# Two stage joints by column pieces, one PSUM pool, and the opening of the last stage in another order

## The chip, the cores and the metric

The kernel runs on one core of a Trainium2 chip. The metric is the device time of one execution in microseconds (us), the median of three runs. Five engines work side by side: PE (TensorE, matmuls; PEld is its weight load), DVE (VectorE), ACT (ScalarE), POOL (GpSimd), and SP, whose queue issues the DMAs. PE writes to PSUM, which has eight banks of 128 x 512 float32.

## The reference

Three layers follow each other; the output of one is the input of the next.

```python
def _attn_ref(r, k, v, w, u):          # 4 batches, 8 heads, 768 steps, 48 wide
    for t in range(S):
        cur = np.einsum('bhd,bhe->bhde', u[None] * kt, vt)
        y[:, :, t] = np.einsum('bhd,bhde->bhe', rt, state + cur)
        state = w[None, :, :, None] * state + np.einsum('bhd,bhe->bhde', kt, vt)
def _moe_ref(x, phi, w1, w2):          # 3072 tokens x 384, 8 experts of 4 slots, F = 1024
    d = softmax of x @ phi over the tokens;  c = softmax of x @ phi over the slots
    slot_input = d.T @ x
    slot_out[e] = np.maximum(slot_input[e] @ w1[e], 0.0) @ w2[e]
    return c @ slot_out
def _moe2_ref(x, w_in, w_out):         # 384 -> 2048 -> 384
    r = np.maximum(x @ w_in, 0.0)
    return (r * r) @ w_out
```

(The two softmax lines are put in words here.)

## The kernel before, in words

The order of every engine's instructions is the order in which the program text emits them (a manual schedule); a wait is put in where two instructions touch the same tile. So what stands earlier in the text on one engine is in front of what stands later, and can hold it up.

**Attention** runs over 16 units (four batches of four head pairs). Its last lines (L890 to L932) are the **first joint**. The last batch's logits lie in the PSUM tile tagged `lg`. Their column maxima over all batches are brought to one row (L900, L902, L903) and spread again (L908, L910), and `fac` (L912, ACT) is the factor by which the sums of earlier batches (`P2[:, 0]`) and of the last one are rescaled. L913 (DVE) rescales `P2[:, 0]`, 385 columns in one instruction; six matmuls for each of three groups of columns (L919) give the last batch's sums, and L921 (DVE, three times) adds them to `P2[:, 1]`. L924 turns the three groups with the 0/1 matrix `sel` into one PSUM tile, L927 copies them as `siT`, and L928 to L932 do the denominators. `turns` (L247 to L276) brings the last unit's outputs into `xn`: the first half of the heads is copied by ACT, the second by DVE (L272). `idle` (L228) issues matmuls whose results nobody reads. Then the PSUM pool is closed and another one opened (L933 to L935).

**The slot stage** (L944 to L1068) does the experts: `up` (L949) reads `siT` in three column groups `kc`, `turn` transposes, `down` (L970) gathers all experts in one PSUM tile `acc`. Beside it DVE rebuilds float32 words of `w_in` and `w_out` (`to_f32`; `wout_f32` in three steps), `wout_high` (ACT, L1009) and `wout_low` (POOL, L1014) split a block of `w_out` into a high and a low part, and `csplit`, `cstack`, `cstack_copy` prepare the slot weights `cTall`.

**The second joint** is L1078 to L1182. `so` is the copy of `acc` (ACT, one instruction), `soT` its product with `sel`. `G(f, ...)` multiplies `soT` with block `f` of `w_in` (128 of its 2048 columns) and stores it in `gst` in a high and a low part (L1097 on ACT, L1098 on DVE). `quarters(q, ...)` does the same for four blocks at once but with 32 rows each (L1106), and eight small transfers on the SP queue per two blocks put their rows into place (`quarters_out`, L1120: four of 16 KB for one block).

**The last stage** is a loop over 96 steps (L1184): three groups of 1024 tokens, 16 blocks `f`, two halves of 512 tokens. For step `i`, `s_h` (L1134) makes the hidden values in PSUM, `s_relu` (ACT, L1145) rectifies them, `s_sq` squares (DVE L1152, or ACT L1150 for steps 2 to 27), `s_hi` (ACT, L1155) rounds the square to its high part `gh`, and `s_lo` (DVE, L1158) leaves the low part `gl`. Nine matmuls of 512 columns (L1229) multiply: three high x `gh`, three low x `gh`, three high x `gl`. `s_h` is issued two steps ahead, `s_hi` and `s_lo` one step ahead. The results leave by L1237 (two halves of 256 columns, ACT and DVE) or, in the last two steps, L1239 (one instruction), and a DMA each (L1240).

```python
    def s_relu(i, c=ALL):
        nc.scalar.activation(fs[i, "hr"][:, c], fs[i, "p"][:, c], AF.Relu)
    def s_hi(i, c=ALL):
        nc.scalar.copy(part(i, "gh")[:, c], fs[i, "gg"][:, c])
    def s_lo(i, c=ALL):
        nc.vector.tensor_tensor(part(i, "gl")[:, c], fs[i, "gg"][:, c], fs[i, "gh"].bitcast(F32)[:, c], ALU.subtract)
```

Of the kernel before, what the change touches and what calls it, by code (L numbers as in the profile page):

```python
# [17 lines left out]
def rwkv_softmoe_ffn(ctx: ExitStack, tc: tile.TileContext, un, wt, ph, w1, w2, w_in, w_out, out):  # L18
# [24 lines left out]
    psum_cm = tc.tile_pool(name="psum_att", bufs=1, space=bass.MemoryType.PSUM)  # L43
    psum = psum_cm.__enter__()
# [3 lines left out]
    BANKS = {"A": 3}  # L48

    def ps(tag, banks=1):  # L50
        cnt[0] += 1
        return psum.tile([128, 512 * banks], F32, name=f"ps_{tag}{cnt[0]}", tag=tag, bufs=BANKS.get(tag, 1))
# [194 lines left out]
    def turns(x, k):  # L247
# [22 lines left out]
        for a in range(2):  # L270
            if x is not None:
                (nc.vector.tensor_copy if a and x == NU - 1 else nc.scalar.copy)(turned(x, a), px[a])  # L272
            if k is not None:
                nc.scalar.copy(kn[:, :4, a], to[a])
# [630 lines left out]
    idle(2, 128, 64)  # L905
    nc.scalar.copy(st["el", B - 1][:, 1], st["lg", B - 1][:96, :256])
# [15 lines left out]
    pv, pd = ps("kv"), ps("lg")  # L922
    for c in range(3):
        nc.tensor.matmul(pv[:, NS * c:NS * (c + 1)], P2[:, 1, 128 * c:128 * (c + 1)], sel[:96, 0],  # L924
                         start=(c == 0), stop=True, skip_group_check=True)
    siT = wk([128, 3, NS], "siT", 1)
    nc.vector.tensor_copy(siT.rearrange("p c s -> p (c s)"), pv[:, :3 * NS])  # L927
# [150 lines left out]
    nc.scalar.copy(so, acc[:, :DM])  # L1078
    cstack(3, "lg")
    wout_f32(2, 0)  # L1080
    p = ps("tr")
    for c in range(3):
        nc.tensor.matmul(p[:, 128 * c:128 * (c + 1)], so[:, 128 * c:128 * (c + 1)], sel.rearrange("p r s -> p (r s)"),
                         start=True, stop=True)
    nc.scalar.copy(soT.rearrange("p c s -> p (c s)"), p[:, :384])
    cstack(4, "kv")
    cstack_copy(3)
    cstack_copy(4, nc.vector.tensor_copy)
    wout_f32(2, 1)
    wout_f32(2, 2)  # L1090

    def G(f, n, tag):
# [3 lines left out]
        g = gst[:, 128 * f:128 * (f + n)]  # L1096
# [63 lines left out]
    G(0, 1, "A")  # L1160
    G(1, 1, "A")
    s_h(0)
    s_h(1)
    G(2, 1, "A")
    quarters(1, "lg")
    first, second = slice(0, 256), slice(256, 512)
    s_relu(0, first)
    s_relu(0, second)
    s_sq(0, first)
    s_hi(0, first)  # L1170
    s_sq(0, second)
    s_lo(0, first)
    s_hi(0, second)
    quarters_high()
    s_relu(1)
    s_lo(0, second)
    quarters_low()
    quarters_out(1, 0)
    s_sq(1)
    G(3, 1, "kv")  # L1180
# [3 lines left out]
    for i, (sg, f, half) in enumerate(order):  # L1184
        if f == 0:
            acc = (acc if half else []) + [[ps(t) for t in atag[half]]]
        if sg == 0 and half == 0:
            wout_f32(f + 3, 0)
        if i + 1 < NI:
            s_hi(i + 1)  # L1190
            s_lo(i + 1)
        if sg == 0 and half == 1:
            wout_f32(f + 3, 1)
        if i + 2 < NI:
            s_h(i + 2)
            s_relu(i + 2)
            s_sq(i + 2)
        if sg == 0 and half == 0:
# [7 lines left out]
        if i in (11, 19):  # L1206
            quarters(2 + i // 19, "tr")
            quarters_high()
            quarters_low()
        for q in range(1, NQ):  # L1210
            at = i - (0, 0, 11, 19)[q]
            if at in ((2, 4, 6) if q == 1 else (0, 2, 4, 6)):
# [88 lines left out]
```

## Time and profile before

| | us |
|---|---|
| median of three runs (376.81 to 377.42) | 377.04 |
| the profiled execution, its own time | 376.01 |
| its span | 374.3 |
| PE busy | 366.4 (98%) |
| DVE busy | 266.6 (71%) |
| ACT busy | 205.4 (55%) |
| POOL busy | 103.7 (28%) |

The span is what the trace covers, and 1.7 us of the execution's own time lie around it. The page gives busy times per engine, the chain that ended last (followed back from the last instruction), and groups of instructions; the trace answers for any stretch which instruction ran when, and what it waited for.

### The profile page before, as it was taken

What the parts mean: (1) busy time and instruction counts of PE and PEld (TensorE: products, weight loads), DVE (VectorE), ACT (ScalarE), POOL (GpSimd) and SP (SyncE); (2) the same over time, 40 slices, a digit from 0 to 9 for tenths busy, and PEclk for the clock granted to TensorE, in tenths of its full rate; (3) what the DMA queues carried; (4) which work ended last, traced back from release to release, by engine and by line L of the source; (5) the groups of instructions that cost most, each with busy time, mean ns of one, the idle gap of its engine ahead of it and who ended that gap; (6) DMA issues with size and microseconds to landing.
All of it is one profiled execution on the core that took longest, in us unless ns stands there. A gap on an engine that the chain in (4) does not pass through costs nothing.

```text
span 374.3 us, 9041 instructions
## 1 busy us (share of the span) xinstructions
PE 366.4 (98%) x3703; PEld 298.7 (80%) x3703; DVE 266.6 (71%) x460; ACT 205.4 (55%) x439; POOL 103.7 (28%) x117
## 2 busy tenths in 40 slices
PE   8999999999999999999999999999999999999995
PEld 6888888988886556887878888888888888888884
DVE  8879878889663694899885767566666765666662
ACT  3244544543632433998887765555555655555553
POOL 3558795587633130352222400000000000000000
PEclk9999999999999999999999999999999999999999
DMA  7999899999999998142332013000000210000004
GB/s 263 411 340 415 301 407 391 406 361 407 332 392 409 409 388 291 34 121 89 106 93 65 7 42 126 3 0 0 2 1 0 100 70 0 2 1 0 2 0 169
DMA packets 22281, 65.09 MB, mean 174 GB/s; under 512 B 2416, under 2 KB 4448, under 8 KB 22240
## 3 DMA queue, kind: packets, MB, share of 16 engines
q1 hardware_dynamic: 22240, 64.52, 46.0%
q8 instruction: 29, 0.48, 0.5%
q14 instruction: 12, 0.10, 0.1%
HBM read 59.00 MB, written 4.72 MB: 170 GB/s over the span
## 4 chain that ended last, share of the span: by engine, by line
PE 97%; DVE 1%; issue 1%; ACT 0%; POOL 0%; POOLq 0%; ACTq 0%
PE ps_A L1229 26%; PE ps_Y L1229 9%; PE ps_kv L1229 9%; PE ps_lg L1229 9%; PE ps_A L306 7%; PE ps_tr L1134 6%; PE ps_YO L336 3%; PE ps_YE L345 3%; PE ps_A L949 3%; PE ps_YO L345 3%; PE ps_Y L970 3%; PE ps_lg L359 2%; PE ps_kv L318 2%; PE ps_YE L269 2%; PE ps_lg L222 1%; PE ps_kv L269 1%
## 5 line engine op out<-in xcount | busy, mean ns | idle before, releaser
L1158 DVE TENSOR_TENSOR slot<-slot,slot 128x512 fp32r<-128x512 f32 (+1 forms) x97 | 71.1, 734 | 53.5 <-PE ps_A L1229 18.6
L1229 PE MATMUL ps_A<-slot,slot 128*128 128x512 f32 x432 | 105.9, 389 | 0.0
L1229 PEld LDWEIGHTS ps_A<-slot,slot 128*128 128x128 f32 x432 | 81.0, 188 | 17.1 <-ACT slot L1155 0.3
L1155 ACT CAST slot<-slot 128x512 fp32r<-128x512 f32 (+1 forms) x97 | 59.7, 616 | 49.5 <-DVE slot L1152 49.1
L1145 ACT ACTIVATE slot<-ps_tr 128x512 f32<-128x512 f32 (+1 forms) x97 | 57.4, 593 | 23.1 <-PE ps_tr L1134 22.1
L1152 DVE TENSOR_TENSOR slot<-slot 128x512 f32<-128x512 f32 (+1 forms) x71 | 48.4, 682 | 11.5 <-ACT slot L1145 11.3
L1229 PE MATMUL ps_Y<-slot,slot 128*128 128x512 f32 x144 | 55.4, 391 | 0.0
L1229 PE MATMUL ps_kv<-slot,slot 128*128 128x512 f32 x144 | 55.1, 389 | 0.0
L1229 PE MATMUL ps_lg<-slot,slot 128*128 128x512 f32 x144 | 55.0, 389 | 0.0
L311 DVE COPY_PREDICATED AT<-mask,ps_A 128x384 f32<-128x384 int32 x63 | 33.6, 586 | 7.5 <-PE ps_A L306 3.2
L1134 PE MATMUL ps_tr<-slot,slot 128*128 128x512 f32 x96 | 37.4, 391 | 0.4 <-DVE slot L1098 0.4
L1014 POOL TENSOR_TENSOR slot<-wf,slot 128x384 fp32r<-128x384 f32 x16 | 20.6, 1288 | 53.2 <-ACT slot L1009 53.2
L295 POOL TENSOR_SCALAR_AFFINE_SELECT AT<-dg 128x768 f32<-128x768 f32 x32 | 28.0, 880 | 20.3 <-DVE dg L288 8.1
L1229 PEld LDWEIGHTS ps_Y<-slot,slot 128*128 128x128 f32 x144 | 27.0, 188 | 5.9 <-issue 0.4
L1229 PEld LDWEIGHTS ps_kv<-slot,slot 128*128 128x128 f32 x144 | 27.0, 188 | 5.7
L1229 PEld LDWEIGHTS ps_lg<-slot,slot 128*128 128x128 f32 x144 | 27.0, 188 | 5.5
L306 PE MATMUL ps_A<-slot 48*128 48x128 f32 x378 | 30.3, 288 | 0.0
L236 DVE TENSOR_TENSOR slot<-slot,ps_tab 112x768 f32<-112x768 f32 (+1 forms) x34 | 29.8, 891 | 0.0
L306 PEld LDWEIGHTS ps_A<-slot 48*128 48x128 f32 x378 | 24.5, 187 | 4.9 <-issue 3.2
L1134 PEld LDWEIGHTS ps_tr<-slot,slot 128*128 128x128 f32 x96 | 17.9, 188 | 4.3 <-DVE slot L1098 0.6
L284 POOL TENSOR_TENSOR slot<-slot,slot 128x576 f32<-128x576 f32 x13 | 18.4, 1417 | 7.6 <-ACT slot L276 7.5
L348 ACT COPY xT<-ps_YE 112x384 f32<-112x384 f32 x16 | 7.7, 479 | 23.4 <-PE ps_YE L345 23.4
(208 smaller groups left out, 529.1 us busy)
## 6 DMA issues: line engine op xcount, KB each, us to landing
slot<-in_un_dram SPq DMA_DIRECT2D x12, 1344.0 KB, 7.3
slot<-in_w_dram SPq DMA_DIRECT2D x24, 512.0 KB, 8.5
slot<-in_w_dram SPq DMA_DIRECT2D x8, 1536.0 KB, 9.7
slot<-in_w_in_dram SPq DMA_DIRECT2D x4, 1536.0 KB, 8.8
wo<-in_w_out_dram SPq DMA_DIRECT2D x16, 384.0 KB, 3.3
out_dram<-slot SPq DMA_DIRECT2D x18, 256.0 KB, 2.4
slot<-in_un_dram SPq DMA_DIRECT2D x9, 448.0 KB, 6.5
slot<-slot SPq DMA_DIRECT2D x48, 16.0 KB, 1.8
```

The lines of the kernel that those rows point to most:

```text
L236: nc.vector.tensor_tensor(x, x, t.unsqueeze(1).to_broadcast(list(x.shape)), ALU.mult)
L295: nc.gpsimd.affine_select(out=at, in_=dg.unsqueeze(3).to_broadcast([128, 2, HC, 128]), pattern=[[0, 2], [0, HC], [1, 128]], compare_op=ALU ...
L306: nc.tensor.matmul(p[h][:, i], tv[rows, 1, 2 * i + par], tv[rows, 0, 2 * i + par], start=True, stop=True)
L311: nc.vector.copy_predicated(st[n, "AT", par][:, h], mask.unsqueeze(1).to_broadcast([128, HC, 128]), p)
L345: nc.tensor.matmul(p[o:o + D, i], vv[:, 2 * i + par, h], at[:, h, i], start=False, stop=True, skip_group_check=True)
L1014: nc.gpsimd.tensor_tensor(wout_half(wls, f, 5), st.pop(("wf", f)), hi, ALU.subtract)
L1134: nc.tensor.matmul(p, gst[:, 128 * f:128 * (f + 1)], cTall[:, 512 * g:512 * (g + 1)], start=True, stop=True)
L1145: nc.scalar.activation(fs[i, "hr"][:, c], fs[i, "p"][:, c], AF.Relu)
L1152: nc.vector.tensor_mul(gg, hr, hr)
L1155: nc.scalar.copy(part(i, "gh")[:, c], fs[i, "gg"][:, c])
L1158: nc.vector.tensor_tensor(part(i, "gl")[:, c], fs[i, "gg"][:, c], fs[i, "gh"].bitcast(F32)[:, c], ALU.subtract)
L1229: nc.tensor.matmul(o, (hi, lo, hi)[k][:, 128 * j:128 * (j + 1)], (gh, gh, gl)[k], start=(f == 0 and k == 0), stop=(f == NF - 1 and k == 2))
```

## The change

First joint: `xn`'s first half is copied by DVE and its second by ACT (before: the other way round). One of two `idle` matmuls before L908 is left out. `P2[:, 0]` is rescaled by ACT in three column groups; the copy of the logits (L906) is moved behind that. The three `sel` products go to three PSUM tiles and are copied one by one by ACT. There is one PSUM pool for the whole kernel: the tag `tr` of the later stages takes the banks `YE` and `YO` in turn, `Y` takes the bank `tab`.

Second joint: `so` and `soT` are made in three pieces. Only blocks 0 and 1 come from `G`; blocks 2 and 3 now come from `quarters(0)` and eight small transfers, and `quarters(1)` moves from the joint into step 3 of the loop. `G` is split: the store of block 1 (`G_out`) comes after step 0's rectifying. `cstack_copy(4)` moves from DVE to ACT and to a later place, `wout_f32(2, 1)` and `(2, 2)` to later places. Step 0: DVE writes the high part straight from the rectified values while ACT makes the square (`s_first`), and its first three matmuls are split into two halves of 256 columns. Step 2's `s_h`, `s_relu` and `s_sq` (`s_ahead`) come between the matmuls of step 0, and in later steps ahead of `wout_high`.

End: the last output tile leaves in two halves (ACT and DVE).

```diff
-    idle(2, 128, 64)
-    nc.scalar.copy(st["el", B - 1][:, 1], st["lg", B - 1][:96, :256])
+    idle(1, 128, 64)
...
-    nc.vector.tensor_scalar(P2[:, 0], P2[:, 0], fac[:, 0:1], None, ALU.mult)
     cols = [slice(0, 128), slice(128, 256), slice(256, DM + 1)]
+    siT = wk([128, 3, NS], "siT", 1)
+    for c in cols:
+        nc.scalar.activation(P2[:, 0, c], P2[:, 0, c], AF.Copy, scale=fac[:, 0:1])
+    nc.scalar.copy(st["el", B - 1][:, 1], st["lg", B - 1][:96, :256])
...
+    for c, tag in enumerate(("kv", "lg", "A")):
+        p = ps(tag)[:, :NS]
+        nc.tensor.matmul(p, P2[:, 1, 128 * c:128 * (c + 1)], sel[:96, 0], start=True, stop=True)
+        nc.scalar.copy(siT[:, c], p)
+    pd = ps("kv")
...
+    for c in range(3):
+        nc.scalar.copy(so[:, 128 * c:128 * (c + 1)], acc[:, 128 * c:128 * (c + 1)])
...
+        p = ps("A")[:, :128]
+        nc.tensor.matmul(p, so[:, 128 * c:128 * (c + 1)], sel.rearrange("p r s -> p (r s)"), start=True, stop=True)
+        (nc.scalar.copy if c == 1 else nc.vector.tensor_copy)(soT[:, c], p)
...
+    def s_first(c):
+        nc.vector.tensor_mul(part(0, "gh")[:, c], fs[0, "hr"][:, c], fs[0, "hr"][:, c])
+        nc.scalar.activation(fs[0, "gg"][:, c], fs[0, "hr"][:, c], AF.Square)
...
+    G(0, 1, "Y")
+    wout_f32(2, 1)
+    quarters(0, "lg")
     s_h(0)
     s_h(1)
...
+    G(1, 1, "Y")
     s_relu(0, first)
     s_relu(0, second)
...
+    s_first(first)
+    s_first(second)
+    G_out(1)
+    s_relu(1)
     s_lo(0, first)
...
+    s_lo(0, second)
+    s_sq(1)
     quarters_high()
...
     quarters_low()
...
+    quarters_out(0, 2)
+    quarters_out(0, 3)
+    cstack_copy(4)
+    wout_f32(2, 2)
     wout_high(1)
     wout_low(1)
...
-        if i in (11, 19):
-            quarters(2 + i // 19, "tr")
+        if i in (3, 11, 19):
+            quarters(1 + (3, 11, 19).index(i), "tr")
...
+        if i == 0:
+            for c in (first, second):
+                for j in range(NJ):
+                    nc.tensor.matmul(acc[0][j][:, c], hi[:, 128 * j:128 * (j + 1)], gh[:, c], start=(c is first),
+                                     stop=False, skip_group_check=True)
+            mms = mms[NJ:]
...
+            if i == 0 and k == 2 and j == 0:
+                s_ahead(2)
...
-                if i < NI - 2:
+                if i < NI - 2 or (i == NI - 1 and j == NJ - 1):
```

PE's order at the first joint, in the kernel before, from the spreading of the maxima (`m`) to the first `up`; lines carry the numbers of their own program, and numbers behind a name count tiles:

```order
L908 MATMUL ps_kv_2067<-ones,m_193_2055 96x2
L919 MATMUL ps_YE_116<-xn_86,en_2061 32x128 x6
L919 MATMUL ps_YO_117<-xn_86,en_2061 32x128 x6
L919 MATMUL ps_A_2074<-xn_86,en_2061 32x129 x6
L924 MATMUL ps_kv_2096<-sel,P_144 128x32 x3
L928 MATMUL ps_lg_2097<-P_144,sel 128x1
L949 MATMUL ps_A_2117<-slot_6_76,siT_2101 32x256 x12
```

The same place in the changed kernel:

```order
L912 MATMUL ps_kv_2065<-ones,m_193_2055 96x2
L926 MATMUL ps_YE_116<-xn_86,en_2061 32x128 x6
L926 MATMUL ps_YO_117<-xn_86,en_2061 32x128 x6
L926 MATMUL ps_A_2076<-xn_86,en_2061 32x129 x6
L931 MATMUL ps_kv_2098<-sel,P_144 128x32
L931 MATMUL ps_lg_2101<-sel,P_144 128x32
L931 MATMUL ps_A_2104<-sel,P_144 128x32
L934 MATMUL ps_kv_2107<-P_144,sel 128x1
L952 MATMUL ps_A_2118<-slot_6_76,siT_2071 32x256 x12
```

The work is the same; the three `sel` products now end in three tiles.

PE's order at the second joint before, from the product that gives `soT` to the first matmul of step 0 (`ps_tr<-slot,slot 128x512` is `s_h`, 32x128 x12 are `quarters`, 128x128 x3 on `slot_220` are `G`):

```order
L1083 MATMUL ps_tr_2440<-sel,slot_258_2428 128x128 x3
L986 MATMUL ps_kv_2445<-ident,cs_2366 128x128 x4
L1095 MATMUL ps_A_2456<-slot_220_2189,slot_258_2428 128x128 x3
L1095 MATMUL ps_A_2462<-slot_220_2189,slot_258_2428 128x128 x3
L1134 MATMUL ps_tr_2468<-slot_234_2256,slot_260_2430 128x512
L1134 MATMUL ps_tr_2470<-slot_234_2256,slot_260_2430 128x512
L1095 MATMUL ps_A_2472<-slot_220_2189,slot_258_2428 128x128 x3
L1106 MATMUL ps_lg_2478<-slot_220_2189,slot_258_2428 32x128 x12
L1095 MATMUL ps_kv_2507<-slot_220_2189,slot_258_2428 128x128 x3
L1134 MATMUL ps_tr_2522<-slot_234_2256,slot_260_2430 128x512
L1229 MATMUL ps_A_2515<-slot_261_2431,slot_253_2384 128x512
```

And in the changed kernel:

```order
L1087 MATMUL ps_A_2449<-sel,slot_260_2429 128x128
L989 MATMUL ps_kv_2452<-ident,cs_2367 128x128 x4
L1095 MATMUL ps_tab_2458<-slot_222_2190,slot_260_2429 128x128 x3
L1110 MATMUL ps_lg_2465<-slot_222_2190,slot_260_2429 32x128 x12
L1138 MATMUL ps_YO_2478<-slot_236_2257,slot_262_2431 128x512
L1138 MATMUL ps_YE_2480<-slot_236_2257,slot_262_2431 128x512
L1095 MATMUL ps_tab_2482<-slot_222_2190,slot_260_2429 128x128 x3
L1244 MATMUL ps_A_2514<-slot_263_2432,slot_255_2385 128x256
```

Two of four `G` products are gone, and one `s_h` stands behind step 0's first matmuls instead of before them.

ACT's order in the changed kernel from step 0's rectifying to step 1's rounding (`L1159`):

```order
L1149 ACTIVATE slot_260_2429<-ps_YO_2478 128x256 x2
L1171 ACTIVATE slot_260_2429<-slot_260_2429 128x256 x2
L1103 CAST slot_262_2431<-ps_tab_2482 128x128
L1149 ACTIVATE slot_260_2429<-ps_YE_2480 128x512
L1115 CAST slot_261_2430<-ps_lg_2465 128x128
L992 CAST slot_236_2257<-ps_kv_2452 128x512
L1012 CAST slot_255_2385<-wf_2389 128x384
L1159 CAST slot_263_2432<-slot_260_2429 128x512
```

The store of block 1 (L1103) and `cstack_copy(4)` (L992) stand between step 0 and step 1 now; the former stood ahead of step 0, the latter on DVE.

## Rows read from the trace of the kernel before

**Rows 1.** The page: the chain that ended last, by engine
```profile
PE 97%; DVE 1%; issue 1%; ACT 0%; POOL 0%; POOLq 0%; ACTq 0%
```
**Rows 2.** Waits of PE inside the span: us in total, times, longest
```profile
PE ps_kv L908 <- DVE m L903: 0.4, 1, 0.4
PE ps_tr L1134 <- DVE slot L1098: 0.4, 1, 0.4
...
PE ps_A L949 <- DVE m L930: 0.2, 1, 0.2
```
**Rows 3.** First joint, timeline: start, us, engine, line, operation, count, idle before
```profile
113.59 0.46 DVE L272 COPY xn<-ps_YO 128x288 f32<-128x288 f32 x1 [0.64 <-ACT xn L272]
113.97 0.23 DVE L902 TENSOR_REDUCE m<-ps_kv 1x32 f32<-1x96 f32 x1
...
115.42 0.42 DVE L913 TENSOR_SCALAR P<-P,m 96x385 f32<-96x385 f32 x1 [0.36 <-ACT m L912]
115.94 0.35 DVE L921 SCALAR_TENSOR_TENSOR P<-ps_YE,m,P 96x128 f32<-96x128 f32 x1
...
116.34 0.93 PE L924 MATMUL ps_kv<-sel,P 96*128 96x32 f32 x6
...
117.72 5.39 PE L949 MATMUL ps_A<-slot,siT 128*32 128x256 f32 x96 [0.25 <-DVE m L930]
```
**Rows 4.** Second joint, timeline of PE, ACT and DVE, from the first G
```profile
144.79 1.60 PE L1095 MATMUL ps_A<-slot,slot 128*128 128x128 f32 x12
...
146.48 0.55 DVE L1098 TENSOR_TENSOR slot<-ps_A,slot 64x128 fp32r<-64x128 f32 x2
...
146.83 0.73 PE L1134 MATMUL ps_tr<-slot,slot 128*128 128x512 f32 x2 [0.43 <-DVE slot L1098]
...
148.26 0.27 ACT L1097 CAST slot<-ps_A 128x128 fp32r<-128x128 f32 x1 [1.56 <-PE ps_A L1095]
148.43 0.67 ACT L1145 ACTIVATE slot<-ps_tr 128x256 f32<-128x256 f32 x2
...
148.89 0.76 DVE L1152 TENSOR_TENSOR slot<-slot 128x256 f32<-128x256 f32 x2
...
150.14 2.35 PE L1229 MATMUL ps_A<-slot,slot 128*128 128x512 f32 x9
...
152.56 0.39 PE L1229 MATMUL ps_Y<-slot,slot 128*128 128x512 f32 x1
```
**Rows 5.** The chain in order of time: start, us; steps 10 and 12
```profile
173.12 2.04 PE ps_A L1229 x9
...
178.69 2.04 PE ps_A L1229 x9
```
**Rows 6.** The transfers of quarters_out on the SP queue, all 48
```profile
L1120 SPq DMA_DIRECT2D slot<-slot x48: 507/588/942, 150.3 to 206.0; - x48
...
DMA to landing us min/median/max: 1.7/1.8/4.3
```
**Rows 7.** Timeline of POOL, then DVE, at two places where both work
```profile
151.40 1.01 POOL L1014 TENSOR_TENSOR slot<-wf,slot 128x384 fp32r<-128x384 f32 x1 [10.82 <-ACT slot L1009]
166.31 1.46 POOL L1014 TENSOR_TENSOR slot<-wf,slot 128x384 fp32r<-128x384 f32 x1 [3.31 <-ACT slot L1009]
...
151.51 0.29 DVE L1098 TENSOR_TENSOR slot<-ps_kv,slot 64x128 fp32r<-64x128 f32 x1
...
165.87 0.68 DVE L1158 TENSOR_TENSOR slot<-slot,slot 128x512 fp32r<-128x512 f32 x1
...
166.81 1.50 DVE L1158 TENSOR_TENSOR slot<-slot,slot 128x512 fp32r<-128x512 f32 x1
```
**Rows 8.** The end: the last copy, and the halved copies of earlier tiles by form
```profile
370.01 0.59 ACT L1239 COPY slot<-ps_kv 128x512 f32<-128x512 f32 x1 [0.82 <-PE ps_kv L1229]
...
L1237 DVE COPY slot<-ps_kv 128x256 f32<-128x256 f32 x2 | 0.8, 416 | 0.0
```
**Rows 9.** Busy times and granted clock (last three: clock, DMA, GB/s), first joint
```profile
114.00:116.00 2.00, 1.56 (x37) 1.45 (x38) 1.02 (x6) 0.63 (x3) 0.00 (x0) 1.00 1.00 412
```

More of the change, by code (lines that the diff above doesn't have):

```diff
@@ L42, in rwkv_softmoe_ffn @@
     att = att_cm.__enter__()
-    psum_cm = tc.tile_pool(name="psum_att", bufs=1, space=bass.MemoryType.PSUM)
-    psum = psum_cm.__enter__()
+    psum = ctx.enter_context(tc.tile_pool(name="psum", bufs=1, space=bass.MemoryType.PSUM))
     ctx.enter_context(tc.manual_schedule())
@@ L271, in turns @@
             if x is not None:
-                (nc.vector.tensor_copy if a and x == NU - 1 else nc.scalar.copy)(turned(x, a), px[a])
+                (nc.vector.tensor_copy if not a and x == NU - 1 else nc.scalar.copy)(turned(x, a), px[a])
             if k is not None:
@@ L1158, in s_lo, with s_ahead @@
         nc.vector.tensor_tensor(part(i, "gl")[:, c], fs[i, "gg"][:, c], fs[i, "gh"].bitcast(F32)[:, c], ALU.subtract)
-    G(0, 1, "A")
-    G(1, 1, "A")
+    def s_ahead(i):
+        s_h(i)
+        s_relu(i)
+        s_sq(i)
+    def s_first(c):
+        nc.vector.tensor_mul(part(0, "gh")[:, c], fs[0, "hr"][:, c], fs[0, "hr"][:, c])
+        nc.scalar.activation(fs[0, "gg"][:, c], fs[0, "hr"][:, c], AF.Square)
+    first, second = slice(0, 256), slice(256, 512)
+    G(0, 1, "Y")
+    wout_f32(2, 1)
+    quarters(0, "lg")
     s_h(0)
     s_h(1)
-    G(2, 1, "A")
-    quarters(1, "lg")
-    first, second = slice(0, 256), slice(256, 512)
+    G(1, 1, "Y")
     s_relu(0, first)
     s_relu(0, second)
-    s_sq(0, first)
-    s_hi(0, first)
-    s_sq(0, second)
+    s_first(first)
+    s_first(second)
+    G_out(1)
+    s_relu(1)
     s_lo(0, first)
-    s_hi(0, second)
+    s_lo(0, second)
+    s_sq(1)
     quarters_high()
-    s_relu(1)
-    s_lo(0, second)
     quarters_low()
-    quarters_out(1, 0)
-    s_sq(1)
-    G(3, 1, "kv")
+    quarters_out(0, 2)
+    quarters_out(0, 3)
+    cstack_copy(4)
+    wout_f32(2, 2)
     wout_high(1)
@@ L1186, in rwkv_softmoe_ffn @@
             acc = (acc if half else []) + [[ps(t) for t in atag[half]]]
-        if sg == 0 and half == 0:
+        if sg == 0 and half == 0 and i:
             wout_f32(f + 3, 0)
@@ L1191, in rwkv_softmoe_ffn @@
             s_lo(i + 1)
+        if i == 0:
+            wout_f32(3, 0)
         if sg == 0 and half == 1:
             wout_f32(f + 3, 1)
[L1194 to L1198, printed above, removed]
+        if 0 < i < NI - 2:
+            s_ahead(i + 2)
+        if sg == 0 and (half == 0 and i or i == 1):
             wout_high(f + 2)
@@ L1226, in rwkv_softmoe_ffn @@
             mms = [(j, k) for j in range(NJ) for k in range(3)]
+        if i == 0:
+            for c in (first, second):
[3 more added lines that the diff above has]
+            mms = mms[NJ:]
         for j, k in mms:
             o = acc[half][j]
+            if i == 0 and k == 2 and j == 0:
+                s_ahead(2)
             nc.tensor.matmul(o, (hi, lo, hi)[k][:, 128 * j:128 * (j + 1)], (gh, gh, gl)[k],
-                             start=(f == 0 and k == 0), stop=(f == NF - 1 and k == 2))
+                             start=(f == 0 and k == 0 and i > 0), stop=(f == NF - 1 and k == 2), skip_group_check=not (sg or half))
             if f == NF - 1 and k == 2:
```

34 lines of the change are left out of this document (14 added, 20 removed).

## Prediction

> **What bounds the kernel now.** I read the page's chain first, then PE's waits, then the timelines of the two joints and the end. The chain is 97% PE [rows 1]: the reader should see that no other engine's speed matters as a whole, only the places where PE stands still or does work that another order would spare it. The waits [rows 2] name such places inside the span: 0.4 us before L908 and 0.2 us before L949 (first joint), 0.4 us before L1134 (second joint). They are small because PE is given other work ahead of the wait; what the change can win is therefore not the sum of waits but the time from one stage's last useful result to the next stage's first matmul. A step of the loop costs PE ten matmuls; the chain shows two steps with a `quarters` between them taking 178.69 - 173.12 = 5.57 us [rows 5], and one 512-column matmul there takes 2.04 / 9 = 0.227 us, so two steps are 20 x 0.227 = 4.53 us and `quarters` inside the loop costs 5.57 - 4.53 = 1.03 us.
>
> **First joint.** Four edits on one path.
> (a) L902 stands behind DVE's copy of `xn`, which had itself waited 0.64 us for ACT's copy; DVE begins at 113.59 and L902 at 113.97 [rows 3]. With the halves swapped DVE copies at once. Its 0.46 us then end at about 113.41 (an estimate: the start moves back by the 0.64 us of waiting), and L902 can start when its row is in PSUM, about 113.55. Gain 0.4 us for L908, the factor and everything behind.
> (b) L913 rescales 385 columns in 0.42 us and L921's first addition starts at 115.94 [rows 3]. Now ACT does 128 columns at a time; the nearest ACT row is the 128x128 store, 0.27 us [rows 4]. So the first addition starts at about 115.94 - 0.4 - 0.15 = 115.4, the third, held by PE's sums, about 0.5 us earlier than before.
> (c) Before, the third `sel` product had to end (116.34 + 0.93 = 117.27), DVE copied all 96 columns and `up` began at 117.72, released last by a DVE read of the closing pool (L930) [rows 2, 3]. Now `up` needs only the first copied piece, which lies ready before the third product; PE goes on when the products and the denominators have been issued, about 0.5 us after the third addition. That gives 116.7 instead of 117.72.
> (d) The `idle` matmul left out and the moved logits copy cost nothing: PE waits for the maxima there anyway, and the copy, 256 columns, is done before the second `sel` product, which reuses its bank. Without that cover it would cost its length, under the 0.59 us of a 512-column copy on ACT [rows 8].
> Sum **-1.0 us**. Ends: -0.5 (only (a) and the pool's release, if the pieces add as much hand-over as they save) and -1.15. I take -1.0, since (a) and (c) alone give it by rows. From `up` to the end of the slot stage PE has no wait (the list shows none there [rows 2]), so the shift arrives at the second joint.
>
> **Second joint**, in times of the trace before, the shift left aside. `G` began at 144.79; `soT` by pieces (three copies of 128 columns instead of one of 384 in front of the next matmul, twice) brings it to about 144.3. L1098 began at 146.48, behind conversions and `cstack_copy(4)` on DVE; these now come after it. What lies ahead of it is one `G` of 0.8 us (half of 1.60), ACT's store of 0.27 and two hand-overs that I put at 0.1 each: 144.3 + 1.3 = 145.6. Step 0's `s_h` follows 0.35 us later, as before (146.83 - 146.48), at 145.95: a gain of 0.9 us [rows 4].
> Then ACT waited 1.56 us for the third `G`, stored it at 148.26 and rectified at 148.43; step 0 began at 150.14 [rows 4]. Now the rectifying follows `s_h` directly, at about 146.4 (a 512-column matmul shows 0.39 us from start to end). DVE writes the high part itself, so that ACT's rounding between DVE's square and PE falls away: the squares start 148.89 - 148.43 = 0.46 us after the rectifying, at 146.86, a half takes 0.38 us (0.76 / 2) [rows 4], and step 0 starts at about 147.3; the one `G` in between ends a little sooner.
> From there ACT and DVE, not PE, set step 1; I lined their instructions up in the changed order, with 0.3 to 0.4 us for one of 256 columns, 0.6 to 0.7 for one of 512 and 0.3 for a block's store (an estimate from [rows 4, 7, 8]). ACT: two squares, the store of block 1, the rectifying of step 1 (ends 148.5), then three more copies; DVE: the second part of block 1's store (from 148.0), two low parts (to 149.0), step 1's square (to 149.65); ACT rounds it by 150.3. Step 1 starts at about **150.34** instead of 152.56 [rows 4]: **-2.2 us**. PE alone could have been there 1 us sooner.
> Against this stand:
> - `quarters(1)` inside the loop: **+1.03 us** [rows 5]. `quarters(0)` takes the place of the one that stood in the joint.
> - The blocks 2 and 3 now come by transfers. `s_h` of step 4 stands on PE ahead of step 2's matmuls, at about 152.4. Its four transfers wait for the copies of `quarters(0)`: the first two may start at 148.7 (ACT), the last two at 149.9 (DVE); at 0.59 us each the fourth starts at 150.5, and 1.8 us later it has landed [rows 6]: 152.35. Just in time; I price 0 to 0.8 us, and the maximum of 4.3 us that the row shows would make it 2.5.
> - The subtraction on POOL (`wout_low(1)`) now falls at 149.6 to 150.6, beside the last conversion on DVE. DVE's subtraction of two tiles in SBUF took 0.68 us once and 1.50 us the next time, beside a POOL subtraction; one that reads PSUM took 0.29 us beside another [rows 7], the same as each of the two in [rows 4] (0.55 for both). So I charge the conversion's delay of up to 0.8 us, which pushes step 1's low part from 151.0 to 151.9, 0.2 us past PE's need at 150.34 + 6 x 0.227 = 151.7.
> Together I take +0.3 for the last two. The Trainium skill (SBUF — State Buffer, section Who interferes with whom) says that DVE and GpSimd share one pair of ports as a lock, and that a DVE instruction with at most one input in SBUF does not take it. By that rule `quarters_low`, which reads PSUM, is not delayed and the joint's sum stays as below; were it blocked for 0.8 us like a subtraction of two SBUF tiles, the transfers would land at 153.1 and the sum would be 0.7 smaller. The trace agrees with the rule at its two places, so I keep the former.
> The halved matmuls: six of 256 columns at half of 0.227 are the same 0.68 us as three of 512. The trace has no such form in this type; the plain float32 one in `up` takes 5.39 / 96 x 4 = 0.225 us for 256 columns (four column strips run side by side [rows 3]), so the bounds are 0.68 and 1.35 us. I take 0.68, the type being that of the loop's matmuls, and keep +0.7 for the range, some of it hidden because step 1 waits for ACT anyway.
> Sum: -2.2 + 1.03 + 0.3 = **-0.9 us**. Ends: -1.2 and +0.9 (transfers at 0.8 more, halves at 0.7, step 1 half a us later).
>
> **The end.** The last copy takes 0.59 us on ACT; a half takes 0.42 on DVE, the slower of the two engines that share it now [rows 8]. **-0.17 us**, ends 0 and -0.2.
>
> **Sum.** -1.0 - 0.9 - 0.17 = -2.07. The profiled execution took 376.01 us (span 374.3, 1.7 around it), so 373.9; the median lies 1.03 above that execution, so I forecast **375.0 us**.
>
> **Rivals.**
> 1. *The transfers come late.* Step 4's `s_h` waits 0.8 to 1.5 us longer than I allow, because the copies that feed the eight transfers sit behind step 1's work on ACT and DVE, and SP issues them one by one. For it: the margin I find is zero. Against: landing is 1.8 us in the median with an idle queue. Time: 375.0 + 1.0 = 376.0. Chance 0.18.
> 2. *The first joint gives half.* If `up` waits for all three copies, or the small ACT instructions cost more than they spare, 0.5 us are lost: 375.6 with the rest unchanged. Against: the waits are put on pieces of `siT`. Chance 0.14, mostly still faster.
> 3. *Slower: the transfers really block.* If the fourth transfer lands as the slowest of the 48 did, 4.3 us after its issue [rows 6], behind a load of `w_out` or the tail of `w_in`, PE stands at step 2 for about 2.5 us, which eats the 2.07; with the conversion's delay in front of ACT's rounding it goes beyond. It decides at a landing of 3.9 us (1.8 + 2.1): 377.5. Against: the loads issued before are over by then and the next one is queued behind the eight transfers. Chance 0.06.
> 4. *Slower: the clock.* PE is busy for 1.56 of 2.00 us in the joint, at a granted clock of 1.00, that is 2.4 GHz [rows 9], and the change takes one `idle` matmul away. Should the clock fall to its lower level of 1.2 GHz there, the first `up` products (5.39 us [rows 3]) would take up to twice as long: 375.0 + 5 = 380. The Trainium skill (TensorE: Matmul & The Clock Gate, HAM oscillation) warns that pauses between bursts of matmuls bring this about. Here the pauses get shorter, so I give it 0.02.
>
> **How the numbers follow.** Forecast 0.60 (374.3 to 375.7), rivals as above. 0.2% of 377 is 0.75 us, about what a measurement of this kernel can tell from no change; faster means below 376.3. The forecast, most of rivals 1 and 2 lie there: 0.78. Between 376.3 and 377.8: late transfers together with a weak first joint, part of rival 3: 0.14. Slower: 0.08. The range must take in rival 1 and the full sum of the gains (-1.15, -1.2, -0.2, so 374.5, and another 0.6 should PE wait less for ACT at step 1): 373.9 to 376.5.
>
> **What would show it.** First joint: `up` starts about 1.0 us earlier, its last releaser no longer L930. Second joint: step 0 starts about 2.8 us earlier counted from the first `cstack` of the joint, step 1 about 2.2. Loop: one more 1.03 us at step 3; a PE wait at step 4's `s_h` released by a DMA would mean rival 1 or 3. End: last copies of 256 columns. A first joint unchanged, or more than 1 us of PE waits between step 0 and step 3, would make me wrong.

## The result and the profile after

The changed kernel takes **374.31 us** (median of five runs, 373.57 to 375.08), the kernel before beside it 377.39: ratio 0.9914, 95% interval 0.9886 to 0.9943. That lies inside the range, 0.7 us below the forecast of 375.0. Run a second time the kernel took 374.45 against 376.44: 0.9936 (0.9911 to 0.9962).

The changed kernel's profiled execution took 374.71 us, its span 373.0 us, with PE busy for 365.9 of it. It is 1.30 us shorter than the profiled execution of before, which is less than the medians say. The first views show why. The page's chain by engine (answering [rows 1]) and the list of PE's waits ([rows 2]), which in both kernels is headed by 1.4 us before PE's very first matmul:

```profile
PE 96%; ACT 1%; DVE 1%; issue 1%; POOL 0%; POOLq 0%; ACTq 0%
```
```profile
PE ps_A L311 <- issue: 0.7, 1, 0.7
PE ps_YE L274 <- issue: 0.3, 1, 0.3
PE ps_kv L912 <- DVE m L908: 0.2, 1, 0.2
```

The two longest of these three are called "issue" (nothing that the profile shows) and lie in the attention, whose instructions did not change there; the attention ended about 1 us later than in the profile of before. So I count from a mark at its end: **R**, the start of DVE's reduction of the last maxima (L366 before, 112.35; L371 now, 113.42). From R the program falls into three lengths: R to `up`'s first matmul (first joint), from there to the start of the last output copy (slot stage, second joint and loop), and from there to the end of the span. Before: 5.37 + 252.29 + 4.29 us. After: 4.68 + 251.21 + 3.67, which is **0.69 + 1.08 + 0.62 = 2.39 us less**.

The first joint of the changed kernel, timeline of all engines, PEld being PE's weight load (answering [rows 3]):

```profile
113.42 0.42 DVE L371 TENSOR_REDUCE nmx<-ps_lg 96x1 f32<-96x256 f32 x1 [1.37 <-PE ps_lg L364]
...
113.98 0.46 DVE L277 COPY xn<-ps_YE 128x288 f32<-128x288 f32 x1
...
115.19 0.30 PE L912 MATMUL ps_kv<-ones,m 1*96 1x2 f32 x2 [0.21 <-DVE m L908]
...
116.48 0.35 DVE L928 SCALAR_TENSOR_TENSOR P<-ps_YE,m,P 96x128 f32<-96x128 f32 x1 [0.80 <-ACT P L920]
...
116.94 0.35 ACT L921 COPY el<-ps_lg 96x256 f32<-96x256 f32 x1
117.06 0.35 DVE L928 SCALAR_TENSOR_TENSOR P<-ps_A,m,P 96x129 f32<-96x129 f32 x1
...
117.34 0.30 PEld L931 LDWEIGHTS ps_lg<-sel,P 96*128 96x128 f32 x2 [0.16 <-ACT el L921]
...
117.58 0.39 PE L931 MATMUL ps_A<-sel,P 96*128 96x32 f32 x2
...
117.81 0.36 PE L934 MATMUL ps_kv<-P,sel 96*128 96x1 f32 x2
...
118.10 2.15 PE L952 MATMUL ps_A<-slot,siT 128*32 128x256 f32 x36
```

DVE copies `xn` without waiting, and `up` has no wait left that the profile shows. But the second `sel` product (117.34) waits for ACT's copy of the moved logits, and PE then issues three more products before `up`.

The second joint and the first steps of the loop (answering [rows 4]):

```profile
144.66 0.83 PE L1095 MATMUL ps_tab<-slot,slot 128*128 128x128 f32 x6
...
146.22 0.50 PE L1138 MATMUL ps_YO<-slot,slot 128*128 128x512 f32 x1
...
147.17 0.76 DVE L1170 TENSOR_TENSOR slot<-slot 128x256 fp32r<-128x256 f32 x2 [0.46 <-ACT slot L1149]
...
147.65 0.98 PE L1244 MATMUL ps_A<-slot,slot 128*128 128x256 f32 x6
148.47 0.86 PE L1251 MATMUL ps_A<-slot,slot 128*128 128x512 f32 x3
...
148.86 3.17 SPq L1124 DMA_DIRECT2D slot<-slot  x5
...
149.22 0.68 DVE L1156 TENSOR_TENSOR slot<-slot 128x512 f32<-128x512 f32 x1
...
149.93 0.29 DVE L1119 TENSOR_TENSOR slot<-ps_lg,slot 128x128 fp32r<-128x128 f32 x1
149.94 0.62 ACT L1159 CAST slot<-slot 128x512 fp32r<-128x512 f32 x1 [0.20 <-DVE slot L1156]
150.14 1.10 DVE L160 SCALAR_TENSOR_TENSOR wf<-wo,wf 128x384 int32<-128x384 int32 x1
...
150.61 0.19 PEld L1251 LDWEIGHTS ps_tab<-slot,slot 128*128 128x128 f32 x1 [0.49 <-ACT slot L1159]
...
152.81 0.40 PE L1138 MATMUL ps_YO<-slot,slot 128*128 128x512 f32 x1
```

Step 0 begins at 147.65 and step 1 at 150.61, released by ACT's rounding (L1159). Step 4's `s_h` at 152.81, which needs the first four transfers, does not wait.

The chain in order of time, steps 2 and 4 of the loop with `quarters(1)` between them (answering [rows 5]), and the end (answering [rows 8]):

```profile
153.21 2.08 PE ps_A L1251 x9
...
158.82 2.04 PE ps_A L1251 x9
```
```profile
369.31 0.37 ACT L1259 COPY slot<-ps_kv 128x256 f32<-128x256 f32 x1 [0.81 <-PE ps_kv L1251]
369.72 0.42 DVE L1259 COPY slot<-ps_kv 128x256 f32<-128x256 f32 x1 [0.43 <-ACT slot L1259]
```

The two halves run one after the other: 0.83 us from start to end where one copy took 0.59. The trace of before had shown this already at the earlier tiles (L1237), which left in halves there too; two lines of its timelines of ACT and DVE:

```profile
223.09 0.37 ACT L1237 COPY slot<-ps_A 128x256 f32<-128x256 f32 x1 [0.31 <-PE ps_A L1229]
...
223.49 0.42 DVE L1237 COPY slot<-ps_A 128x256 f32<-128x256 f32 x1 [0.26 <-ACT slot L1237]
```

In all twelve tiles that leave in halves there, DVE's half begins after ACT's has ended.

### The profile page after: what moved, and what is told of

It reads as the page before. It is cut to its first block, busy times and chain, and to the rows that moved or that the text cites. A ratio compares the mean times of both kernels' runs of the same rounds, so it can differ in the third digit from the quotient of the medians.

```text
span 373.0 us, 9092 instructions
## 1 busy us (share of the span) xinstructions
PE 365.9 (98%) x3716; PEld 297.8 (80%) x3716; DVE 266.4 (71%) x459; ACT 206.9 (55%) x447; POOL 103.1 (28%) x117
## 4 chain that ended last, share of the span: by engine, by line
PE 96%; ACT 1%; DVE 1%; issue 1%; POOL 0%; POOLq 0%; ACTq 0%
PE ps_A L1251 26%; PE ps_tab L1251 9%; PE ps_kv L1251 9%; PE ps_lg L1251 9%; PE ps_A L311 7%; PE ps_YO L341 3%; PE ps_YE L350 3%; PE ps_YO L1138 3%; PE ps_A L952 3%; PE ps_YO L350 3%; PE ps_tab L973 3%; PE ps_YE L1138 3%; PE ps_lg L364 2%; PE ps_kv L323 2%; PE ps_YE L274 2%; PE ps_lg L227 1%
## 5 line engine op out<-in xcount | busy, mean ns | idle before, releaser
L1162 DVE TENSOR_TENSOR slot<-slot,slot 128x512 fp32r<-128x512 f32 (+1 forms) x97 | 70.2, 725 | 53.8 <-PE ps_A L1251 18.5
L1159 ACT CAST slot<-slot 128x512 fp32r<-128x512 f32 x95 | 58.9, 620 | 49.2 <-DVE slot L1156 48.9
L1156 DVE TENSOR_TENSOR slot<-slot 128x512 f32<-128x512 f32 x69 | 47.6, 691 | 11.4 <-ACT slot L1149 11.2
L1251 PE MATMUL ps_tab<-slot,slot 128*128 128x512 f32 x144 | 55.6, 393 | 0.1
L1149 ACT ACTIVATE slot<-ps_YO 128x512 f32<-128x512 f32 (+1 forms) x49 | 28.8, 589 | 12.8 <-PE ps_YO L1138 12.3
L1149 ACT ACTIVATE slot<-ps_YE 128x512 f32<-128x512 f32 x48 | 28.7, 598 | 12.3 <-PE ps_YE L1138 11.7
L1251 PEld LDWEIGHTS ps_tab<-slot,slot 128*128 128x128 f32 x144 | 27.0, 188 | 6.5 <-issue 0.6
L1138 PE MATMUL ps_YO<-slot,slot 128*128 128x512 f32 x48 | 18.8, 392 | 0.0
```

The costliest lines, as they stand in the source:

```text
L1138: nc.tensor.matmul(p, gst[:, 128 * f:128 * (f + 1)], cTall[:, 512 * g:512 * (g + 1)], start=True, stop=True)
L1156: nc.vector.tensor_mul(gg, hr, hr)
```

## The experiments

There is a profile of every kernel here, so all of them can be laid on the same three lengths (us). "Sum" is the difference of the three from before, "median" the difference from the median of before in the same batch. Those medians come from 5 to 35 runs of before, and pass from 376.44 to 377.39 between batches.

| kernel | R at | R to up | up to last copy | last copy to end | sum | median |
|---|---|---|---|---|---|---|
| before | 112.35 | 5.37 | 252.29 | 4.29 | 0 | 0 |
| before, again | 112.55 | 5.37 | 252.29 | 4.29 | 0.00 | 0.0 |
| changed | 113.42 | 4.68 | 251.21 | 3.67 | -2.39 | -3.1 |
| changed, again | 112.21 | 4.67 | 251.21 | 3.67 | -2.40 | -2.0 |
| first joint alone | 112.72 | 4.67 | 252.28 | 3.95 | -1.05 | -1.3 |
| second joint alone | 113.42 | 5.37 | 251.21 | 3.49 | -1.88 | -2.0 |
| last copy whole | 112.32 | 4.67 | 251.18 | 3.48 | -2.62 | -3.1 |
| denominators behind up | 112.77 | 4.39 | 251.66 | 3.67 | -2.23 | -2.4 |
| halves not swapped | 113.41 | 5.13 | 251.21 | 3.66 | -1.95 | -1.9 |
| block 2 transferred last | 112.96 | 4.68 | 255.41 | 3.66 | +1.80 | +1.7 |
| two pools | 113.00 | 5.05 | 251.20 | 3.67 | -2.03 | -2.1 |
| before, eight more transfers | 112.71 | 5.37 | 252.26 | 3.48 | -0.84 | -0.7 |
| siT whole | 113.12 | 4.81 | 251.19 | 3.67 | -2.28 | -2.4 |
| three repairs | 113.93 | 4.58 | 251.83 | 3.48 | -2.06 | -2.3 |

Apart from the changed kernel, whose two medians lie on either side of its sum, sums and medians agree within 0.5 us. The first two lengths come back within 0.03 us in kernels that share the code of the stretch; R wanders over 1.7 us.

### The two kernels again

Edit: none.

> The kernel before, word for word, profiled and timed a second time. Theory A (the trace of before that the prediction used was a quick execution: its attention ends early by chance): the same lengths between marks as in the first trace (5.37 us from the reduction of the maxima to up, 24.90 to the joint's cstack, 227.4 to the last copy), while the reduction itself comes at 112.3 to 113.4 us; time within 0.2% of the other runs of before. Rival: one of the three lengths is 0.5 us or more longer than in the first trace, so that the changed kernel gained that much more than its trace shows.

> The changed kernel, word for word, a second time. Theory A: the lengths between marks of its first trace return (4.68 us to up, 24.90 to the joint's cstack, 226.3 to the last copy, 3.66 to the end), while the reduction of the maxima falls anywhere between 112.3 and 113.4 us; time 2.1 to 2.6 us below before. Rival: one of the lengths differs by over 0.2 us.

Measured: before 376.48 (0.9992, 0.996 to 1.0023), changed 374.45; all lengths return. Theory A holds both times for the lengths: the gain is 2.4 us, and only 1.30 us showed between the first two profiles because R fell 1.07 us later in the second. In the median the changed kernel was 2.0 us below before, 0.1 short of what theory A had.

### The parts alone

Edit of the first: the text of before from L1078 on, under the new first joint. Edit of the second: the other way round, without the halved last copy.

> The kernel before with the first joint's edits alone (pieces, swapped halves, one PSUM pool, one idle matmul fewer); second joint and end as before. Theory A (the sum of the prediction, as the changed kernel's trace resizes it): from DVE's reduction of the maxima to the first matmul of up takes 4.7 us instead of 5.37, and the time is 0.7 us below before. Theory B (the prediction's own size): 4.4 us, time 1.0 below. Rival 2 of the prediction (half of it): 4.9 us, time 0.5 below. Rival C (the one pool is worth more than the trace shows, as the measured -3.2 us is more than the sum): time 1.5 us or more below.

> The kernel before with the second joint's edits alone (G and quarters in the new order, step 0 split, rectifying ahead, quarters(1) inside the loop at step 3, copies by pieces); two pools, first joint and end as before. Theory A (trace of the changed kernel): step 1 starts 2.3 us earlier counted from up's first matmul, quarters(1) gives 1.1 back, time 1.1 to 1.2 below before. Rival 1 (the transfers come late): a wait of 0.8 us or more before step 4's product, time 0.4 below or less. Rival C: the parts help each other, so that this alone gives under 0.5.

Measured: 375.44 (0.9966, 0.9944 to 0.9987) and 374.71 (0.9943, 0.9913 to 0.9972). The middle lengths are those of theory A: the first joint gives 0.70, the second 1.08, and they add up (0.69 and 1.08 together in the changed kernel). Both medians went lower than A, by 0.6 and 0.9. The third length shows where: it shrank too, by 0.34 and 0.80, although neither kernel changes the end. Rival C is not it. The section on the end of the span takes that up. The edits of the second joint were not tried one by one: that they give 1.08 together is shown, and their single prices below are read from the trace.

### The first joint, edit by edit

Halves not swapped: `if not a and` back to `if a and`.

> The changed kernel with ACT and DVE copying the halves of xn as before. Theory A (term (a) of the prediction): from the reduction of the maxima to up's first matmul 5.1 us instead of 4.68, time 0.4 above the changed kernel. Rival (the pieces of P and siT hide it, or PE's sums were the later ones): 4.8 us or less, time the same within 0.1.

Measured: 374.55, R to `up` 5.13. The swap is worth 0.45 us, as theory A has it. The wait is back in the timeline, with PE's wait behind it:

```profile
114.66 0.46 DVE L277 COPY xn<-ps_YO 128x288 f32<-128x288 f32 x1 [0.64 <-ACT xn L277]
...
115.63 0.30 PE L912 MATMUL ps_kv<-ones,m 1*96 1x2 f32 x2 [0.67 <-DVE m L908]
```

Two pools: the tags and the closing of the first pool as before, with the pieces kept.

> The changed kernel with two PSUM pools as before, so that up's bank waits for the last reader of the closed pool again. Theory A (term (c)): up's first matmul then waits for DVE's reading of the denominators, 0.6 us after their product starts instead of 0.29: 5.0 us from the reduction of the maxima, time 0.3 above the changed kernel. Rival (the pool's release was worth nothing, the pieces alone give it): 4.7 us, time the same.

Measured: 374.39, R to `up` 5.05: the one pool is worth 0.37, as theory A has it. `up` waits again:

```profile
117.78 0.16 DVE L932 TENSOR_SCALAR m<-ps_kv 128x1 f32<-128x1 f32 x1 [0.79 <-PE ps_kv L930]
...
118.05 2.32 PE L951 MATMUL ps_A<-slot,siT 128*32 128x256 f32 x37 [0.30 <-ACT siT L928]
```

The profile names ACT, but ACT's last copy had ended at 117.78. DVE's read of the denominators in the closing pool ended at 117.94, 0.11 us before `up`; in the kernel before it ended 0.06 us before `up`. So I put the wait down to that read. This is argued from the times, not named by the profile.

`siT` whole:

```diff
-    for c, tag in enumerate(("kv", "lg", "A")):
...
+    nc.vector.tensor_copy(siT.rearrange("p c s -> p (c s)"), pv[:, :3 * NS])
```

> The changed kernel with siT copied whole by DVE from one bank, as before; the pieces of P, the swap and the one pool stay. Theory A (the pool and the pieces are two releasers of the same matmul, so that each alone gives little): from the reduction of the maxima to up 4.9 us instead of 4.68, time 0.2 above the changed kernel. Rival (the pool alone gives it, the pieces nothing): 4.7 us or less, time the same within 0.1.

Measured: 374.02, R to `up` 4.81, between theory and rival; `up` waits 0.15 us for the one copy:

```profile
117.93 2.37 PE L952 MATMUL ps_A<-slot,siT 128*32 128x256 f32 x40 [0.15 <-DVE siT L933]
```

The pieces of `siT` are worth 0.13 us with the one pool, net of the logits' copy, which holds up the second `sel` product only with the pieces (0.10, next run). With two pools they may even cost: the kernel with all pieces needs 5.05 there, while before less the swap would need 5.37 - 0.45 = 4.92. That is an estimate; it takes the swap to be worth the same 0.45 there, and it holds all the other edits of the joint too. The prices of the swap, the pool and the pieces, 0.45, 0.37 and 0.13, add up to more than the joint's 0.69, since the pool and the pieces release the same matmul.

Denominators behind `up(0)`: the copy of the moved logits stands behind `siT`'s, the second `sel` product takes the bank `tab`, and L934 moves behind the matmuls of `up(0)`.

> The changed kernel with two things moved off PE's path in the first joint: ACT's copy of the moved logits goes behind the copies of siT, with the second sel product on another bank, and the product of the denominators goes behind the matmuls of up(0). Theory A (the shortfall of term (c), 0.31 us of the predicted 1.0, lies in these two): from the reduction of the maxima to up's first matmul 4.25 us instead of 4.68, and up(0) to the end as before plus 0.2 for the moved product: time 0.2 to 0.4 us below the changed kernel. Rival (up's first matmul then waits for the first copied piece of siT instead): 4.5 us or more, time the same within 0.1.

Measured: 374.31, R to `up` 4.39, but the next length grew by 0.45: the product costs more between two `up`s than ahead of them. The sum is 0.16 worse than the changed kernel's. Neither theory was right: theory A's 0.29 us of the shortfall did come off the first joint, but moving the product does not recover it. The three repairs below keep only the move of the copy: 4.58, so that copy costs 0.10.

### The transfers' margin

```diff
-    quarters_out(0, 2)
     quarters_out(0, 3)
+    quarters_out(0, 2)
```

> The changed kernel with the four transfers of block 3 issued ahead of those of block 2, which step 4's product waits for; nothing else moved. Theory A (no margin, as the prediction found): block 2 lands four issues of 0.6 us later, PE waits 2.2 to 2.4 us at step 4's product, behind step 1, and the time is 2.3 us above the changed kernel. Rival (a transfer's data is there well before the landing that the trace shows, margin of 1 us or more): a wait under 1.4 us.

Measured: 378.19 (1.0029, 1.0001 to 1.0058), slower than before the change. In PE's timeline the wait is as theory A has it, 2.42 us; the time is not:

```profile
154.92 0.55 PE L1138 MATMUL ps_YO<-slot,slot 128*128 128x512 f32 x1 [2.42 <-DMA slot<-slot]
...
155.27 1.05 PE L1251 MATMUL ps_A<-slot,slot 128*128 128x512 f32 x2
...
158.88 0.40 PE L1138 MATMUL ps_YE<-slot,slot 128*128 128x512 f32 x1
```

The last of the eight issues (one every 0.64 us) began at 152.9 and its data was used 2.0 us later. The fourth began at 150.3, so in the changed order data is there at 152.3; `s_h` would stand at 150.14 + 2.20 = 152.34 in this run (step 1's start, and the distance of 152.81 from 150.61 in the changed kernel). The margin is 0.0 us, as the prediction found.

But the length grew by 4.2 us, not by 2.4. The windows show the rest (last three columns: granted clock, DMA share, GB/s):

```profile
154.00:155.00 1.00, 0.08 (x1) 0.11 (x2) 1.00 (x2) 0.00 (x0) 0.55 (x1) 1.00 0.60 72
155.00:156.00 1.00, 1.00 (x3) 0.82 (x4) 1.00 (x3) 0.49 (x1) 0.00 (x0) 0.59 0.68 261
156.00:157.00 1.00, 1.00 (x4) 0.71 (x4) 0.44 (x1) 0.97 (x3) 0.00 (x0) 0.50 0.68 154
157.00:158.00 1.00, 1.00 (x4) 0.81 (x3) 0.28 (x1) 0.69 (x2) 0.76 (x1) 0.50 0.78 261
158.00:159.00 1.00, 1.00 (x5) 0.68 (x3) 1.00 (x2) 0.00 (x0) 0.25 (x1) 0.71 0.14 55
```

After PE's standstill the clock was granted at 0.50, its lower level of 1.2 GHz, until within the 158 to 159 us window, and step 2's nine matmuls took 3.6 us (155.27 to step 5's `s_h` at 158.88) instead of 2.08. These 1.5 us are most of the 1.8 that came on top of the wait. The prediction had the long transfer and the clock as two rivals; here the one brings the other.

### The end of the span

```diff
-                if i < NI - 2 or (i == NI - 1 and j == NJ - 1):
+                if i < NI - 2:
```

> The changed kernel with the last copy of the last tile whole again, on ACT. Prediction's term: the halves gain 0.17 us, so this is 0.17 slower than the changed kernel. Rival (its trace: DVE's half waits for ACT's half, 0.37 + 0.42 us one after the other against one copy of 0.59): the last copy ends 0.2 us earlier after PE's last matmul, and the time is 0 to 0.3 us below the changed kernel, unless the landing of the last transfer (2.0 to 3.8 us in the traces) hides it.

Measured: 373.67 (0.9908, 0.9874 to 0.9943), the lowest median of all; the end takes 3.48 instead of 3.67. The halves cost 0.19 us, as the rival says.

What shortened the end of kernels that leave it alone? In the DMA view of before from 369 us on, one load of code (8 KB, on an instruction queue) stands among the outputs, and the outputs land 2.8 us after their issue in the median:

```profile
q14 instruction: 1, 0.01, 0.5%
...
out_dram<-slot SPq DMA_DIRECT2D x3, 256.0 KB, 2.8
```

The kernel before a second time and the one with the first joint alone have it too (2.8 and 2.5 us). The changed kernel and all that have the new second joint do not, and land in 2.0 to 2.1. So the cause should be something that the second joint counts differently. It has 56 `quarters` transfers instead of 48. The test: before, with eight transfers doubled that nobody waits for.

```diff
                 quarters_out(q, at // 2)
+        if i in (5, 7):
+            quarters_out(1, i // 2)
```

> The kernel before with eight more transfers of 16 KB on SP's queue, far from any path: the blocks 2 and 3 of the second quarter sent a second time, with the same data, one step after the first time. Theory A (the end gains because the code load of 8 KB, which the profile shows during the last outputs in every kernel with 48 such transfers and in none with 56, is one of SP's own and moves with the number of its issues): no load on the instruction queues after 369 us, the last output lands 2.0 to 2.1 us after its issue instead of 2.8, the last copy starts 3.5 us before the end of the span instead of 4.29, and the time is 0.6 to 0.8 us below before. Rival (the second joint's order or the number of instructions of PE or ACT decides it): landing 2.5 us or more, 4.0 us or more, time the same as before.

Measured: 375.76 against 376.44, ratio 0.9979 (0.9956 to 1.0001); the last length 3.48, and in the same view no load:

```profile
q1 hardware_dynamic: 734, 1.32, 57.0%
...
out_dram<-slot SPq DMA_DIRECT2D x4, 256.0 KB, 2.1
```

The trace shows it plainly: 0.81 us, in a length that is 4.29 in both profiles of before. The times alone do not settle it, since their interval takes in 1. The load has moved, too. Before has none on this queue between 297 and 300 us; the kernel with eight more transfers has one there:

```profile
q14 instruction: 1, 0.01, 0.7%
```

So doing *more* transfers shortened the end, with the load out of the way: the three profiles with 48 transfers have the load behind 369 us and the late landing, the eleven with 56 have neither. SP issues the last outputs at the same distances from the last copy in before and in this kernel, within 0.1 us; what is late is their landing. That the load brings SP's own instructions is argued from this, not shown, and how 8 KB can delay the outputs stays open.

### Three repairs together

The last copy whole, the logits' copy moved, and for step 1 as for step 0 DVE writes the high part (`s_first(1, ALL)`), so that ACT's rounding falls away.

> The changed kernel with three repairs: the last copy whole, the copy of the moved logits behind siT's with the second product on another bank, and step 1's high part written by DVE as in step 0. Theory A: 0.2 at the end, 0.1 in the first joint (4.57 us to up), 0.2 at step 1 (step 1 starts 2.8 instead of 2.96 us after step 0): 0.4 to 0.5 below the changed kernel, about 0.3 below the kernel with the last copy whole. Rival (step 4's product, which has no margin, then waits for the transfers): 0.2 of it is lost again as a wait for a DMA there, and the time is 0.3 below the changed kernel.

Measured: 374.13 (0.9937, 0.9914 to 0.9961). The changed kernel beside it had 374.45 (0.9936), so the medians show no difference; by the lengths this kernel is 0.34 us worse. Two repairs hold (4.58; 3.48). The third moved step 1 forward, to 150.79 - 148.06 = 2.73 us behind step 0 instead of 2.96, yet the length grew by 0.62. Timeline of DVE, SP, POOL and PE:

```profile
149.93 2.49 SPq L1124 DMA_DIRECT2D slot<-slot  x4
...
150.89 1.09 POOL L1017 TENSOR_TENSOR slot<-wf,slot 128x384 fp32r<-128x384 f32 x1 [9.02 <-ACT slot L1012]
...
151.02 1.51 DVE L1162 TENSOR_TENSOR slot<-slot,slot 128x512 fp32r<-128x512 f32 x1
```
```profile
152.58 0.50 PE L1252 MATMUL ps_tab<-slot,slot 128*128 128x512 f32 x1 [0.27 <-DVE slot L1162]
...
153.77 0.47 PE L1138 MATMUL ps_YO<-slot,slot 128*128 128x512 f32 x1 [0.23 <-DMA slot<-slot]
```

ACT's square of step 1 now stood ahead of `quarters_high`, so the transfers began 1.87 us behind step 0 instead of 1.21 (148.86 - 147.65), and the margin of zero became the rival's wait. And DVE's subtraction of step 1's low part fell beside POOL's and took 1.51 instead of 0.68 us, for which PE waited 0.27. The kernel with the last copy whole stays the best that was run.

## Why the prediction was right, and where it was off

The times of the changed kernel are given here on the clock of before: less 1.07 us in the first joint (R's shift), and from `up` on less 0.38 (118.10 - 117.72), which leaves the first joint's gain aside as the prediction did.

**What bounds the kernel.** PE, and only places where it stands still or works for nothing: right. All that was gained or lost from R on in the 14 profiles lies in PE's order or its waits, except at the end of the span and where the clock fell in one run.

**(a) The swap**, predicted 0.4: measured 0.45.

**(b) P2 in pieces**: the first addition was forecast at 115.4 and came at 116.48 - 1.07 = 115.41.

**(c) `up` at 116.7** failed by 0.33: it came at 117.03. The step that failed is "about 0.5 us after the third addition": that addition ended on time, at 116.34 (its row of before ends at 116.81, and 0.5 less was forecast), and PE needed 0.69 us from there: 0.17 to the third product, 0.23 to the denominators, 0.29 to `up`. About 0.1 of the miss is the prediction's own arithmetic, as 0.5 us behind that end is 116.8 and not 116.7. Another 0.10 is **(d)**, the moved logits' copy that "costs nothing": done "before the second `sel` product" was wrong, PE's weight load waited 0.16 for it. The joint gave 0.69 of the predicted 1.0. It is rival 2 in part, though not by its mechanism: `up` waited for no copy.

**Second joint.** G at 144.66 - 0.38 = 144.28 (forecast 144.3), step 0 at 147.27 (147.3), step 1 at 150.23 (150.34): the line-up of ACT and DVE instruction by instruction held to about 0.1 us, ACT's rounding being the last releaser. `quarters(1)` in the loop: two steps took 158.82 - 153.21 = 5.61 us, that is 1.08 where 1.03 was forecast. The halved matmuls took 148.47 - 147.65 = 0.82 us, nearer the lower bound of 0.68 than 1.35. The +0.3 for transfers and POOL was not paid as a wait: the data came as `s_h` stood ready. The conversion beside POOL was indeed drawn out (L160, 1.10 us), but step 1's low part was in time. Counted from `up`, step 1 starts 2.33 us earlier (2.2 forecast) but step 4's `s_h` only 2.17: step 1 took 0.16 more than in before, most of it at its first matmul (0.34 to the next one instead of 0.23). No term stood for that. -2.33 + 0.16 + 1.08 is the joint's -1.08 within 0.01, where -0.9 was forecast.

**The port rule.** `quarters_low`, which reads PSUM, took 0.29 us with POOL's subtraction beginning 0.12 us before its start; the subtraction of two SBUF tiles in the last run took 1.51. By the rule of the Trainium skill (SBUF — State Buffer, Who interferes with whom) the first is free and the second is not; both agree. The prediction left out that this section of the Trainium skill makes an exception for DVE's 2-port modes, which by the same section a `tensor_tensor` does not have.

**The end** failed in both directions. -0.17 for the halves became +0.19: the engines were taken to share the tile, but the second half waits for the first, as the halves in the trace of before had done. And the 0.81 us that the outputs gain by landing earlier stood in no sum; as far as the prediction goes it is luck. The net is -0.62.

**Rivals.** 1 and 3 did not happen, but rival 3's mechanism is real and stronger than priced: 2.42 us of wait and 1.8 us more behind it, most of it by the lower clock. Rival 4 at the first joint did not happen: the granted clock is 1.00 from 112 to 120 us in all 14 profiles. The Trainium skill (TensorE: Matmul & The Clock Gate, HAM oscillation) puts such a fall down to pauses between bursts of matmuls, and the run with block 2 last agrees in kind: 0.50 granted after a wait of 2.42 us.

**Sum.** Forecast -1.0 - 0.9 - 0.17 = -2.07; measured -0.69 - 1.08 - 0.62 = -2.39. From the profiled 376.01 that leads to 373.6; the two medians lie 0.7 and 0.8 above it, where the prediction added 1.03. So of the 0.7 us between forecast and median about half is the sum (+0.31 in the first joint, -0.18 in the second, -0.45 at the end), and half the step to the median. That the total lies so near is in part luck: the terms were off in both directions, by +0.31 (first joint), -0.18 (second joint), +0.36 (halves) and -0.81 (landing of the outputs), and the last of these was not forecast at all.

## What to carry to other kernels

Line up two engines instruction by instruction where a joint is short: it forecast the starts of both steps within about 0.1 us, whereas the one place where "PE goes on about 0.5 us later" stood in for the line-up was off by 0.3. Compare two traces from a mark behind the stretch that wanders by chance, length by length; a gain of 0.1 us is then plain in a single profile. When two waits release the same instruction, price them together (one pool alone, pieces alone, both), and look at a transfer's margin before moving anything ahead of its issue: at a margin of zero, an issue that came 0.66 us later against step 0 (1.87 instead of 1.21) made PE wait 0.23 us. And before halving a copy over two engines, look whether halves that the kernel already has run side by side.

## What had not been expected of the hardware

- With a load of code among the last outputs they landed 0.4 to 0.8 us later, and eight more small transfers elsewhere moved the load away (end of the span 4.29 to 3.48 us). How the one delays the other stays open.
- A PE wait of 2.42 us cost 4.2: the granted clock fell to 0.50 as work began again, and stayed there until within the fourth us.
- Two copies of the halves of one PSUM tile to one SBUF tile, on ACT and on DVE, ran one after the other (DVE stood idle 0.43 us until ACT's semaphore released it). So the program's own wait puts them in order; whether they would run side by side without it was not tried.
- The attention ends anywhere between 112.21 and 113.93 us in 14 profiles, with "issue" gaps of 0.2 to 0.8 us at different places in most of them, and with PE's first twelve matmuls taking 4.26 to 5.49 us. As the lengths behind R come back within 0.03 us, most of the spread between profiles of one kernel lies here; what sets it stays open.
